# A sixth second-stage product at two levels of Strassen, in a TransNormer attention and StarReLU MLP kernel

## The chip, the cores and the metric

The kernel runs on one core of one Trainium2 chip, in float32 throughout. The metric is the device time of one execution in microseconds (us); a time given is the median of several runs. Five engines with queues of their own work side by side: TensorE (PE) multiplies matrices and writes PSUM, VectorE (DVE) and ScalarE (ACT) do elementwise work, GpSimd (POOL) a little of the set-up, and SyncE (SP) issues nearly all transfers. Each runs its own list of instructions in order, and semaphores make one list wait for another.

## The reference

Batch 8, 8 heads, 576 positions, 64 columns per head, so 4608 tokens of 512 columns; the hidden width is 2048.

```python
kv = einsum('bhsd,bhse->bhde', k, v)
o = einsum('bhsd,bhde->bhse', q, kv)
o = o / sqrt(mean(o * o, axis=-1) + 1e-6) * g_norm
x = o.transpose(0, 2, 1, 3).reshape(4608, 512)
h = x @ w_in                       # 4608x512 @ 512x2048
g = s * max(h, 0)**2 + b
out = g @ w_out                    # 4608x2048 @ 2048x512
```

## The kernel before

The tokens are cut into nine units (U = 9, u from 0) of four chunks of 128 tokens. A unit has a first stage (h and its square, transposed, so that the hidden width lies on partitions), a second stage (the product with w_out), and, between the steps of both, the attention of the following unit.

**First stage (`mm1`).** From unit 1 on it is one level of Strassen-Winograd: seven products in place of eight, for each of NS = 4 blocks s of the hidden width. The products are named x1, z2, x6, y7, x5, x3, y4 after the PSUM bank that they use (x, y, z) and their number. They use sums of the blocks of x (`x_sums`, tiles xs_4 to xs_7) and of w_in (kept from the start). `keep` copies a bank to SBUF on ACT; `relu_sq` squares the positive part on DVE in one operation. For the last block (s = 3) x3 and y4 are put off into the second stage.

**Second stage (`mm2`).** It is also one level of Strassen-Winograd: the products 1 to 7 are of blocks of g (a11, a12, a21, a22 and sums of them, by `G_OF`) with 1024x256 blocks of w_out or sums of those (`w2_dram`). Each is 256 tokens (j = 0, 1 of 128) by 1024 by 256. A direct product (`product`) is eight matrix products of 128x256 for each j, accumulated in one bank. From unit 2 on the products in `TWICE` (1, 2, 6, 7, 4) are split once more by Strassen-Winograd (`second_level`): seven small products m1 to m7, each four matrix products of 128x128, which the trace shows as eight. Their sums of g are made by DVE (`sums`, four 128x512 operations; tiles "sub", eight buffers), their sums of w_out were made once in unit 1 by `parts_of_w` and stored in `w3_dram`. `keep` and `scaled` (line 707) read a bank on DVE, multiply by s and add what is there already. Products 5 and 3 are direct: `x5_of(j)` and `x3(j)`, and both stay in the same x bank, which x5 begins and x3 later ends.

Names of the steps: `p6[3]` is small product m3 of product 6, with its reading. `p4` has product T4 with block a22 of g; its banks are the two of `ps_t` (t_ps) and z. `s2` and `s4` turn g's tiles into Strassen's S2 and S4 in place (S4 stands where a12 was). `with_7` adds product 7 to o2's right half. The results are o1 and o2 (two tiles of 128 tokens each), left and right halves of 256 columns.

**The order of the work** is written out by hand: `rest` lists the second stage in program order, for all engines at once, so the place of a call sets its place in each engine's list. `at(key)` puts in what `sides` gives to that place: steps of the next unit's attention (`turn` transposes q on DVE, `product`, `row_sum`, `norm`, `turn_x`), the loads of q (`loads`, or `loads_in_parts` to spread them), and the sums of x for the next unit. `first[(s, n)]` are places in the first stage, `second[...]` in the second.

**The weights of the second stage** go through a ring of seven tiles. `queue_w2` lists the loads in order, `pump(k)` issues the next k on SP, each into the tile that was used seven places earlier. A direct product has two tiles of 512 KB; a split one has four (2, 2, 2 and 1 of the seven blocks), used in the order 1 2 | 6 7 | 5 3 | 4 (`ORDER`). In units with a batch due, k and v also come through the ring (four tiles).

**SP** takes all of it in program order: ring loads, q, k and v, the stores of w_out's sums in unit 1, and the stores of the results (`store`: four transfers for a tile of 128 tokens, two of them in the first units).

Lines of the profile that matter: 91 (every product), 247 and 250 (additions and subtractions), 409 (transpose of q), 440 (attention product), 547 and 626 (squares on DVE), 592 (`keep` on ACT), 676 and 679 (ring loads, split and direct), 707 (readings), 723 (stores of w_out's sums), 811 (stores of results), 1214 and 1225 (loads of q).

Of the kernel before, what the change touches and what calls it, by code (L numbers as in the profile page):

```python
# [9 lines left out]
FP32 = mybir.dt.float32  # L10
# [6 lines left out]
def kernel(  # L17
# [39 lines left out]
    nc = tc.nc  # L57
# [191 lines left out]
    def sub(o, a, b):  # L249
        nc.vector.tensor_tensor(out=o, in0=a, in1=b, op=ALU.subtract)  # L250
# [38 lines left out]


    w2_dram = [dram.tile([P, FC // 2, HN], FP32, name=f"w2_{i}") for i in range(8)]
    TWICE = (1, 2, 6, 7, 4)
    w3_dram = {
        i: dram.tile([P, 7, FC // 4, P], FP32, name=f"w3_{i}") for i in TWICE
    }
# [212 lines left out]
    def x_sums(u):  # L508
        b11, b12 = xT[u][:, :KH, :TB], xT[u][:, :KH, TB:]
        b21, b22 = xT[u][:, KH:, :TB], xT[u][:, KH:, TB:]  # L510
        for i in (5, 7, 6, 4):
            xs[u, i] = xp.tile([P, KH, TB], FP32, name=f"xs_{i}", tag=f"xs_{i}")

        def t12():
            sub(xs[u, 5], b12, b11)
            sub(xs[u, 6], b22, xs[u, 5])

        def t34():
            sub(xs[u, 7], b22, b12)
            sub(xs[u, 4], b21, xs[u, 6])  # L520

        return t12, t34
# [23 lines left out]
    def relu_sq(t):  # L546
        nc.vector.scalar_tensor_tensor(t, t, 0.0, t, ALU.max, ALU.mult)  # L547
# [38 lines left out]
    def mm1(u, s):  # L586

        st = {}

        def keep(name, src, tag):  # L590
            st[name] = rp.tile([P, 2, TB], FP32, name=name, tag=tag)
            nc.scalar.copy(st[name], src)  # L592

        def x1():
            st["x"] = bank_of("x", "x")
            mm1_product(1, u, s, st["x"], True)
            keep("r1", st["x"], "ra")

        def z2():
            ps = bank_of("z", "z", 1)  # L600
            mm1_product(2, u, s, ps, True)
            t = g_tile("a11", s)
            add(t, ps, st["r1"])
            relu_sq(t)

        def x6():
            mm1_product(6, u, s, st["x"], False)
            keep("r2", st["x"], "rb")

        def y7():  # L610
            st["y"] = bank_of("y", "y")
            mm1_product(7, u, s, st["y"], True)

        def x5():
            mm1_product(5, u, s, st["x"], False)
            keep("r4", st["x"], "ra")
            t = g_tile("a22", s)
            add(t, st["y"], st["r4"])
            relu_sq(t)

        def x3():
            mm1_product(3, u, s, st["x"], False)
            nc.scalar.activation(g_tile("a21", s), st["x"], AF.Relu)  # L623

        def x3_square():
            nc.vector.tensor_mul(ga["a21", s], ga["a21", s], ga["a21", s])  # L626

        def x3_s1():
            g_tile("s1", s)
            g_s1(s)  # L630

        def x3_s3():
            sub(ga["a21", s], ga["a11", s], ga["a21", s])

        def y4():
            mm1_product(4, u, s, st["y"], False)
            add(g_tile("a12", s), st["y"], st["r2"])

        def y4_square():
            relu_sq(ga["a12", s])  # L640

        return dict(
            x1=x1, z2=z2, x6=x6, y7=y7, x5=x5, x3=x3, x3_square=x3_square, x3_s1=x3_s1,
            x3_s3=x3_s3, y4=y4, y4_square=y4_square,
        )
# [13 lines left out]
    queue_w2 = []  # L659
    for u in range(1, U):  # L660
        queue_w2 += [(u, "kv", n) for n in range(NP if u in kv_due else 0)]
        for i in ORDER if u == 1 else (1, 2, 5, 6, 7, 3, 4):
            queue_w2 += [(u, i, n) for n in range(4 if twice(u, i) else 2)]

    def pump(k):
# [21 lines left out]
    def mm2(u, step=None, side={}):  # L687
# [185 lines left out]
            if last(j):  # L873
                store("o2", j, 4 * u + 2 + j, slice(HN, DM))

        def x3(j, *between):
            product(3, j, st["x", j], False)
            for fn in between:
                fn()
            if u > 1:  # L880
                add(right("o1", j), right("o1", j), b_21)
            scaled(rows("o1", j)[:, HN:], st["x", j], b2 if u == 1 else st["o1", j][:, HN:])
            store("o1", j, 4 * u + j)

# [42 lines left out]
        if u == 1:  # L927
            return [
                seq(lambda: x1(0), lambda: parts_of_w(1)),
                seq(lambda: x1(1), lambda: pump(2), s2),  # L930
                seq(lambda: z2(0), lambda: parts_of_w(2)),
                seq(lambda: z2(1), lambda: pump(2), s4),
                seq(lambda: x6(0), lambda: parts_of_w(6)),
                seq(lambda: x6(1), lambda: pump(2)),
                seq(lambda: y7(0), lambda: parts_of_w(7)),
                seq(lambda: y7(1), lambda: pump(2)),
                lambda: x5(0),
                seq(lambda: x5(1), lambda: pump(2)),
                lambda: x3(0),
                seq(lambda: x3(1), lambda: pump(2)),  # L940
                seq(lambda: y4(0), lambda: parts_of_w(4)),
                seq(lambda: y4(1), lambda: pump(2)),
            ]
# [11 lines left out]
            4, lambda j, q: st["r2"][:, j, q], lambda j, q: rows("o2", j)[:, q], "t", "t"  # L955
        )

        def x5_of(j, *between):
            st["x", j] = half(("x", j), "x")
            product(5, j, st["x", j], True)  # L960
            for fn in between:
                fn()
            scaled(right("o2", j), st["x", j], b_21)

        def with_7(j):

            add(right("o2", j), right("o2", j), st["r2"][:, j])
            if last(j):
                store("o2", j, 4 * u + 2 + j, slice(HN, DM))

        def y4_of(j, m):
            p4[m]()
            if last(j):
                store("o2", j, 4 * u + 2 + j, slice(0, HN), (nc.sync, nc.scalar))
            else:
                store("o2", j, 4 * u + 2 + j)

        def rest():
            p1[1]()
            p1[2]()  # L980
            pump(1)
            step["y4"]()
            p1[6]()
            step["y4_square"]()
            p1[7]()
            pump(1)
            p1[5]()
            step["x3"]()
            p2["sums"]()
            p1[3]()  # L990
            pump(1)
            step["x3_square"]()
            p1[4]()
            pump(1)
            at(0)
            p2[1]()
            step["x3_s1"]()
            p2[2]()
            pump(1)
            p2[6]()  # L1000
            step["x3_s3"]()
            p2[7]()
            pump(1)
            s2((0, 1))
            p2[5]()
            x5_of(0, lambda: s2((2, 3)), lambda: p6["sums"]((5, 6)))
            p2[3]()
            pump(1)
            p2[4]()
            pump(1)  # L1010
            at(1)
            x5_of(1, lambda: p6["sums"]((7, 3)), lambda: p7["sums"]((5, 6, 7)))
            pump(2)
            at(2)
            p6[1]()
            s4((0,))
            p6[2]()
            pump(1)
            p6[6]()
            s4((1,))  # L1020
            p6[7]()
            pump(1)
            p6[5]()
            s4((2,))
            st["r2"] = rp.tile([P, 2, HN], FP32, name="or2", tag="rb")
            p7[1]()
            p6[3]()
            pump(1)
            s4((3,))
            p6[4]()  # L1030
            pump(1)
            p7[2]()
            pump(1)
            p7[6]()
            p7[7]()
            pump(1)
            p7[5]()
            at(3)

            def between():  # L1040
                p7["sums"]((3,))
                p4["sums"]()
                at("sums")
                p7[3]()
                pump(1)
                p7[4]()
                pump(1)
                at(("q", 0))
                p4[1]()
                at("norm")  # L1050

            x3(0, between)
            p4[2]()
            p4[6]()
            with_7(0)
            p4[7]()
            with_7(1)
            p4[5]()
            at(4)
            at(5)  # L1060
            x3(1)
            pump(4)
            at(("q", 1))
            y4_of(0, 3)
            pump(1)
            y4_of(1, 4)
            pump(1)
            at(("q", 2))

        return {"sums": p1["sums"], "rest": rest}  # L1070
# [181 lines left out]
    def sides(u):  # L1252
# [34 lines left out]
        else:  # L1287
# [17 lines left out]
                })  # L1305
            else:
                first[2, 0] = [*turn_x[:2], turn[2]]
                first.update({
                    (2, 1): [product[2], row_sum[2]],
                    (2, 2): [norm[2]],  # L1310
                    (2, 3): [turn_x[2], turn[3], *q[1]],
                    (3, 0): [product[3], row_sum[3]],
                    (3, 1): [norm[3]],
                    (3, 2): [turn_x[3]],
                })
        second[5] = [lambda: [sums() for sums in x_sums(u + 1)]]
        return first, second

    for u in range(U):
# [90 lines left out]
```

## Time and profile before

| what | value |
|---|---|
| median of five runs | 954.52 us (952.37, 952.76, 954.52, 955.12, 955.15) |
| the profiled execution's own time | 955.12 us |
| its span | 953.3 us |
| matrix products on TensorE | 7270 |
| mean share of the 16 DMA engines in q1, SP's queue | 54.1% |
| read from and written to HBM | 131.34 MB and 25.95 MB |
| first and last start of TensorE's part in the sixth unit's second stage | 605.63 us and 653.26 us |
| one unit, start of the seventh less start of the sixth | about 100.9 us |

The span is the part of the time that the profiler sees; 1.8 us of this execution lie around it. Busy times of TensorE are modelled and overlap, so the starts of its instructions are the thing to read: the distance between the starts of two groups is what the first costs. A figure in brackets at the end of a line is the time that the engine stood idle just before it, and what ended that. On SP's queue a line's length is the time to issue, not to transfer.

### The profile page before, as it was taken

How to read it: one execution, taken by the hardware profiler on the slowest of the kernel's cores; microseconds unless marked ns; L12 is line 12 of the kernel's file. 1: busy time of each engine (PE TensorE's matmuls, PEld its weight loads, DVE VectorE, ACT ScalarE, POOL GpSimd, SP SyncE). 2: the span in 40 equal slices, each digit the busy share in tenths (PEclk: the TensorE clock that was granted, in tenths of full speed). 3: DMA queues.
4: the chain of work that ended last, by engine and by line, in shares of the span. 5: the costliest groups of instructions: out<-in, count | busy, mean ns of one | idle time of the engine just before them, and what ended most of it. 6: DMA issues, size and time to landing. Idle time of an engine off the chain costs nothing.

```text
span 953.3 us, 17795 instructions
## 1 busy us (share of the span) xinstructions
PE 937.3 (98%) x7270; PEld 840.4 (88%) x7270; DVE 640.1 (67%) x1167; ACT 191.6 (20%) x366; POOL 6.7 (1%) x18
## 2 busy tenths in 40 slices
PE   7999999999999999999999999999999999999997
PEld 7888888888889998889889988999889988998996
DVE  2789667485558765876478656775678567864683
ACT  3684132101221013200231013101320032001100
POOL 2000000000000000000000000000000000000000
PEclk9999999999999999999999999999999999999999
DMA  9588727578762758165644764375526520653064
GB/s 262 185 316 248 249 78 196 136 232 251 211 169 59 245 141 222 22 193 189 178 110 128 240 180 111 92 241 168 154 56 219 189 80 11 221 184 104 26 221 129
DMA packets 136656, 158.46 MB, mean 166 GB/s; under 512 B 77696, under 2 KB 91776, under 8 KB 136448
## 3 DMA queue, kind: packets, MB, share of 16 engines
q1 hardware_dynamic: 133472, 155.57, 54.1%
q10 hardware_dynamic: 2784, 1.77, 0.8%
q8 instruction: 57, 0.93, 0.4%
q14 instruction: 23, 0.19, 0.1%
q0 software_dynamic: 320, 0.00, 0.0%
HBM read 131.34 MB, written 25.95 MB: 165 GB/s over the span
## 4 chain that ended last, share of the span: by engine, by line
PE 87%; DVE 5%; DMA 4%; ACT 2%; issue 1%; SPq 0%; DVEq 0%; ACTq 0%
PE x_ps L91 40%; PE y_ps L91 25%; PE z_ps L91 8%; PE t_ps L91 8%; PE x_ps L440 3%; DMA w_sb<-w 2%; PE kv_ps L377 2%; DMA w_raw<-in_moe_w_in_dram 1%; ACT xT L494 1%; DMA kv_sb<-in_k_dram 1%; DVE xT L488 1%; DVE a L247 1%; DVE a L547 1%; DVE xn L463 1%; DVE sub L250 0%
## 5 line engine op out<-in xcount | busy, mean ns | idle before, releaser
L592 ACT COPY r<-x_ps 128x512 f32<-128x512 f32 x96 | 56.0, 584 | 406.2 <-PE x_ps L91 384.0
L91 PE MATMUL x_ps<-xs,ws 128*128 128x256 f32 x512 | 122.1, 381 | 0.8 <-ACT r L592 0.4
L91 PE MATMUL y_ps<-xs,wb 128*128 128x256 f32 x512 | 122.6, 382 | 0.3 <-DVE a L247 0.3
L91 PEld LDWEIGHTS x_ps<-xs,ws 128*128 128x128 f32 x512 | 96.4, 190 | 15.9 <-ACT r L592 2.9
L91 PEld LDWEIGHTS y_ps<-xs,wb 128*128 128x128 f32 x512 | 95.5, 190 | 16.1 <-DVE a L247 2.6
L247 DVE TENSOR_TENSOR a<-y_ps,r 128x512 f32<-128x512 f32 x64 | 43.9, 686 | 72.2 <-ACT r L592 60.1
L91 PE MATMUL x_ps<-xT,wa 128*128 128x256 f32 x384 | 89.8, 380 | 0.1
L91 PEld LDWEIGHTS x_ps<-xT,wa 128*128 128x128 f32 x384 | 72.2, 190 | 10.5 <-issue 0.6
L91 PE MATMUL x_ps<-w_sb,a 128*128 128x256 f32 (+1 forms) x376 | 80.0, 365 | 0.8 <-DMA w_sb<-w 0.8
L91 PEld LDWEIGHTS x_ps<-w_sb,a 128*128 128x128 f32 x376 | 66.8, 190 | 9.6 <-DMA w_sb<-w 1.2
L547 DVE SCALAR_TENSOR_TENSOR a<-a 128x512 f32<-128x512 f32 x96 | 66.4, 692 | 3.1
L91 PE MATMUL y_ps<-w_sb,sub 128*128 128x128 f32 x504 | 62.0, 275 | 0.0
L91 PEld LDWEIGHTS y_ps<-w_sb,sub 128*128 128x128 f32 x504 | 60.2, 192 | 0.7
L91 PE MATMUL x_ps<-xT,ws 128*128 128x256 f32 x256 | 60.5, 379 | 0.0
L91 PE MATMUL z_ps<-xT,wa 128*128 128x256 f32 x256 | 60.5, 379 | 0.0
L91 PE MATMUL x_ps<-w_sb,s 128*128 128x256 f32 x256 | 58.2, 380 | 1.3 <-DMA w_sb<-w 1.3
L91 PE MATMUL t_ps<-w_sb,sub 128*128 128x128 f32 x448 | 54.8, 275 | 0.0
L91 PEld LDWEIGHTS z_ps<-xT,wa 128*128 128x128 f32 x256 | 48.6, 190 | 6.6
L91 PEld LDWEIGHTS x_ps<-w_sb,s 128*128 128x128 f32 x256 | 47.4, 190 | 7.9 <-DMA w_sb<-w 1.2
L626 DVE TENSOR_TENSOR a<-a 128x512 f32<-128x512 f32 x32 | 22.1, 690 | 47.9 <-ACT a L623 47.9
L91 PE MATMUL y_ps<-w_sb,a 128*128 128x128 f32 (+1 forms) x360 | 53.7, 298 | 0.0
L91 PEld LDWEIGHTS x_ps<-xT,ws 128*128 128x128 f32 x256 | 48.1, 190 | 6.3
(139 smaller groups left out, 1267.2 us busy)
## 6 DMA issues: line engine op xcount, KB each, us to landing
w_sb<-w SPq DMA_DIRECT2D x147, 512.0 KB, 4.8
w_sb<-w SPq DMA_DIRECT2D x35, 256.0 KB, 2.8
w_raw<-in_moe_w_in_dram SPq DMA_DIRECT2D x8, 1024.0 KB, 7.3
w_raw<-in_moe_w_out_dram SPq DMA_DIRECT2D x8, 1024.0 KB, 5.2
w_sb<-in_k_dram SPq DMA_DIRECT2D x48, 144.0 KB, 2.9
w_sb<-in_v_dram SPq DMA_DIRECT2D x48, 144.0 KB, 3.0
out_dram<-o SPq DMA_DIRECT2D x104, 64.0 KB, 2.6
w<-sub SPq DMA_DIRECT2D x20, 256.0 KB, 4.3
```

The source lines that it names most:

```text
L91: nc.tensor.matmul(o, lhsT=lhsT, rhs=rhs, start=start, stop=stop, skip_group_check=True)
L247: nc.vector.tensor_tensor(out=o, in0=a, in1=b, op=ALU.add)
L377: nc.tensor.matmul(ps[r][l * HB : l * HB + HB, i, :], lhsT=kv[l][rows, 0, j, :], rhs=kv[l][rows, 1, j, :], start=(j == 0), stop=(j == R - 1),)
L440: nc.tensor.matmul(ps[32 * p : 32 * p + 32, w, :], lhsT=st["qT"][:, p, 32 * w : 32 * w + 32], rhs=bd_kv[(b if w < 2 else b1) % 2][:, p, :] ...
L463: nc.vector.tensor_tensor(out=st["xn"].rearrange("p h d -> p (h d)").rearrange("p (c h e) -> p h c e", c=KC, h=H), in0=st["x"].rearrange(" ...
L488: nc.vector.transpose(out=to, in_=st["xn"].rearrange("p h d -> p (h d)").rearrange("p (c x) -> p c x", c=KC))
L494: nc.scalar.activation(to[:, i], to[:, i], AF.Copy, scale=g_col[:, i : i + 1])
L547: nc.vector.scalar_tensor_tensor(t, t, 0.0, t, ALU.max, ALU.mult)
L592: nc.scalar.copy(st[name], src)
L626: nc.vector.tensor_mul(ga["a21", s], ga["a21", s], ga["a21", s])
```

## The change

- Product 3 (S4 with block B22 of w_out) joins `TWICE`: in unit 1 `parts_of_w(3)` makes and stores its sums; from unit 2 on it is split in seven (`p3`, banks x, y and z). The order of the ring is ... 7, 4, 3, so product 4 comes ahead of product 3, and product 5 no longer stays in its bank: `with_5` adds it from o2's right half, where `x5_of` puts it.
- The sums of products 4 and 3 (and the last of 7) are no longer made in one run but one or two at a time between the readings, and `s4` is grouped otherwise.
- In the last block of the first stage, from unit 2 on, the two squares are done by ACT, and a21's is ahead of p2's sums.
- The two pairs of `x_sums` are at two places (5 and 6).
- In the last unit the results are stored by halves for both j: o2's right and o1's left half after `with_7(j)`, o2's left after `p4[4]`, o1's right after `p3[3]` and `p3[4]`, on SP and ACT in turn.
- In unit 3 the transpose of the fourth chunk comes ahead of the third's product, the row sum one place later, and the second half of q's loads is in four parts.

```diff
-    TWICE = (1, 2, 6, 7, 4)
+    TWICE = (1, 2, 6, 7, 4, 3)
...
         def t12():
+            tiles(5, 6)
             sub(xs[u, 5], b12, b11)
             sub(xs[u, 6], b22, xs[u, 5])
 
         def t34():
+            tiles(7, 4)
             sub(xs[u, 7], b22, b12)
             sub(xs[u, 4], b21, xs[u, 6])
...
             add(t, st["y"], st["r4"])
-            relu_sq(t)
+            if u > 1 and s == NS - 1:
+                nc.scalar.activation(t, t, AF.Relu)
+                nc.scalar.square(t, t)
+            else:
+                relu_sq(t)
...
         def x3_square():
-            nc.vector.tensor_mul(ga["a21", s], ga["a21", s], ga["a21", s])
+            if u > 1 and s == NS - 1:
+                nc.scalar.square(ga["a21", s], ga["a21", s])
+            else:
+                nc.vector.tensor_mul(ga["a21", s], ga["a21", s], ga["a21", s])
...
-        for i in ORDER if u == 1 else (1, 2, 5, 6, 7, 3, 4):
+        for i in ORDER if u == 1 else (1, 2, 5, 6, 7, 4, 3):
...
-        def x3(j, *between):
+        def x3(j):
             product(3, j, st["x", j], False)
-            for fn in between:
-                fn()
-            if u > 1:
-                add(right("o1", j), right("o1", j), b_21)
...
-                lambda: x3(0),
+                seq(lambda: x3(0), lambda: parts_of_w(3)),
...
+        p3 = second_level(3, lambda j, q: right("o1", j, q), lambda j, q: right("o1", j, q), "x")
...
+        def with_5(j):
+
+            add(right("o1", j), right("o1", j), right("o2", j))
+
         def with_7(j):
 
             add(right("o2", j), right("o2", j), st["r2"][:, j])
-            if last(j):
+            if u == U - 1:
                 store("o2", j, 4 * u + 2 + j, slice(HN, DM))
...
+                store("o1", j, 4 * u + j, slice(0, HN))
+
+        def store_o2(j):
+            store("o2", j, 4 * u + 2 + j, slice(0, HN if u == U - 1 else DM))
+
+        def store_o1(j):
+            cols, queues = (slice(HN, DM), (nc.sync, nc.scalar)) if u == U - 1 else (slice(0, DM), (nc.sync, nc.sync))
+            store("o1", j, 4 * u + j, cols, queues)
...
             step["x3"]()
+            step["x3_square"]()
             p2["sums"]()
...
             p6[1]()
-            s4((0,))
             p6[2]()
...
-            s4((1,))
             p6[7]()
             pump(1)
+            s4((0, 1))
             p6[5]()
+            st["r2"] = rp.tile([P, 2, HN], FP32, name="or2", tag="rb")
             s4((2,))
...
+            p7["sums"]((3,))
+            p4["sums"]((5,))
             p7[5]()
+            p4["sums"]((6,))
             at(3)
-
-            def between():
-                p7["sums"]((3,))
-                p4["sums"]()
-                at("sums")
-                p7[3]()
-                pump(1)
-                p7[4]()
-                pump(1)
-                at(("q", 0))
-                p4[1]()
-                at("norm")
-
-            x3(0, between)
+            p4[1]()
+            p7[3]()
+            pump(1)
+            with_5(0)
+            p7[4]()
+            pump(1)
+            at("sums")
+            p4["sums"]((7,))
+            at(("q", 0))
             p4[2]()
+            pump(1)
             p4[6]()
+            at("norm")
+            p4[7]()
+            pump(1)
+            p4["sums"]((3,))
+            p3["sums"]((5,))
+            p4[5]()
+            with_5(1)
+            p3["sums"]((6,))
+            p3[1]()
+            at(4)
+            p4[3]()
+            pump(1)
+            at(("q", 1))
+            p3["sums"]((7,))
+            p3[2]()
+            p3[6]()
+            p3[7]()
+            p3["sums"]((3,))
             with_7(0)
-            p4[7]()
+            p3[5]()
             with_7(1)
-            p4[5]()
-            at(4)
             at(5)
-            x3(1)
-            pump(4)
-            at(("q", 1))
-            y4_of(0, 3)
-            pump(1)
-            y4_of(1, 4)
-            pump(1)
+            p4[4]()
+            for j in range(2):
+                store_o2(j)
+            pump(3)
+            p3[3]()
+            store_o1(0)
+            pump(1)
+            p3[4]()
+            store_o1(1)
+            pump(1)
+            at(6)
             at(("q", 2))
...
                 first[2, 0] = [*turn_x[:2], turn[2]]
+                parts = loads_in_parts(5, 1, 4)
+                second["q", 0], second["q", 1] = [parts[2]], [parts[3]]
                 first.update({
-                    (2, 1): [product[2], row_sum[2]],
-                    (2, 2): [norm[2]],
-                    (2, 3): [turn_x[2], turn[3], *q[1]],
+                    (2, 1): [turn[3], product[2]],
+                    (2, 2): [row_sum[2], norm[2], *parts[:2]],
+                    (2, 3): [turn_x[2]],
...
-        second[5] = [lambda: [sums() for sums in x_sums(u + 1)]]
+        second[5], second[6] = [[lambda n=n: x_sums(u + 1)[n]()] for n in range(2)]
```

More of the change, by code (lines that the diff above doesn't have):

```diff
@@ L510, in x_sums, with tiles @@
         b21, b22 = xT[u][:, KH:, :TB], xT[u][:, KH:, TB:]
-        for i in (5, 7, 6, 4):
-            xs[u, i] = xp.tile([P, KH, TB], FP32, name=f"xs_{i}", tag=f"xs_{i}")
+        def tiles(*which):
+            for i in which:
+                xs[u, i] = xp.tile([P, KH, TB], FP32, name=f"xs_{i}", tag=f"xs_{i}")
         def t12():
+            tiles(5, 6)
             sub(xs[u, 5], b12, b11)
@@ L963, in x5_of @@
             scaled(right("o2", j), st["x", j], b_21)
+        def with_5(j):
+            add(right("o1", j), right("o1", j), right("o2", j))
         def with_7(j):
             add(right("o2", j), right("o2", j), st["r2"][:, j])
-            if last(j):
+            if u == U - 1:
                 store("o2", j, 4 * u + 2 + j, slice(HN, DM))
[L971 to L976, printed above, removed]
+                store("o1", j, 4 * u + j, slice(0, HN))
[4 more added lines that the diff above has]
+            store("o1", j, 4 * u + j, cols, queues)
         def rest():
@@ L991, in rest @@
             pump(1)
-            step["x3_square"]()
             p1[4]()
@@ L1019, in rest @@
             p6[6]()
-            s4((1,))
             p6[7]()
             pump(1)
+            s4((0, 1))
             p6[5]()
+            st["r2"] = rp.tile([P, 2, HN], FP32, name="or2", tag="rb")
             s4((2,))
-            st["r2"] = rp.tile([P, 2, HN], FP32, name="or2", tag="rb")
             p7[1]()
```

## The prediction

> **What bounds the kernel now.** I read the page first (which engine is full), then TensorE's timeline of one steady unit, then its few waits, then the SP queue at the end. Measurement tells about 0.2% (1.9 us) from no change.
>
> Page, part 1, and part 4:
> ```profile
> PE 937.3 (98%) x7270; PEld 840.4 (88%) x7270; DVE 640.1 (67%) x1167; ACT 191.6 (20%) x366; POOL 6.7 (1%) x18
> ...
> PE 87%; DVE 5%; DMA 4%; ACT 2%; issue 1%; SPq 0%; DVEq 0%; ACTq 0%
> ```
> TensorE is the bound: anything it no longer streams is gained, if nothing makes it wait.
>
> Timeline of TensorE, sixth unit (start, us, engine, operation):
> ```profile
> 636.53 2.84 PE L91 MATMUL y_ps<-w_sb,sub 128*128 128x128 f32 x24
> 639.21 3.62 PE L91 MATMUL x_ps<-w_sb,a 128*128 128x256 f32 x16
> 642.67 1.05 PE L91 MATMUL y_ps<-w_sb,sub 128*128 128x128 f32 x8
> ```
> The printed lengths overlap; starts count. One row tile of the direct third product takes 642.67 - 639.21 = 3.46 us, three small products 639.21 - 636.53 = 2.68, so one "slot" is 0.893 us. No gap lies between: this unit has no wait.
>
> Timeline of TensorE, the waits (in brackets) of the fourth and ninth units:
> ```profile
> 386.17 1.99 PE L91 MATMUL x_ps<-xs,ws 128*128 128x256 f32 x8 [0.39 <-ACT r L592]
> 388.76 1.08 PE L440 MATMUL x_ps<-bd_kv,qT 128*32 128x128 f32 x32 [0.60 <-DVE qT L409]
> ...
> 416.84 1.97 PE L91 MATMUL x_ps<-w_sb,s 128*128 128x256 f32 x8 [0.54 <-DMA w_sb<-w]
> 419.60 1.99 PE L91 MATMUL x_ps<-w_sb,s 128*128 128x256 f32 x8 [0.80 <-DMA w_sb<-w]
> ...
> 934.25 1.99 PE L91 MATMUL x_ps<-w_sb,a 128*128 128x256 f32 x8 [0.85 <-DMA w_sb<-w]
> ```
> These 3.18 us are nearly all the waits in seven two-level units.
>
> SP's queue, fourth unit and end; TensorE's last product:
> ```profile
> 373.70 38.28 SPq L1214 DMA_DIRECT2D q_sb<-in_q_dram  x64
> ...
> 946.50 4.55 SPq L811 DMA_DIRECT2D out_dram<-o  x10
> ```
> ```profile
> 946.67 1.06 PE L91 MATMUL t_ps<-w_sb,a 128*128 128x128 f32 x8
> ```
> The 64 loads of q block SP until 411.98, when ring loads due from about 402.9 go out; that is the wait of 416 to 420. At the end TensorE is done at 946.67 + 0.89 = 947.56, the span only at 953.3: 5.74 us of tail. SP issues ten stores at 0.455 us each up to 951.05, and 2.25 us later all has ended.
>
> **The parts and their cost**, against the profiled execution (span 953.3, its time 955.12; the median is 0.6 lower).
>
> *1. The product.* Direct: 2 x 3.455 = 6.91 us. At two levels: 7 x 0.893 = 6.25. Gain 0.66 in each of seven units: **-4.6 us**. It lies on the path wholly.
>
> *2. DVE.* Per unit four sums (0.60 to 0.72 from start to start), seven readings of 128x128 (0.35) instead of two of 128x256 (0.48), two additions of o2 in place of two of b_21 (0.42 both): 2.7 + 2.45 - 0.96 = +4.2; two squarings (0.69 each) go to ACT, so +2.8 of about 101 us, at 67% busy. ACT gets three 0.59 us operations for it and is 20% busy. What matters is when. I laid DVE's list in the new order beside the slots, counting from p6[1]; a reading starts 0.20 after its product ends (t_ps, 647.13 to 647.33). p4[1] is slot 12, p3[1] slot 19, p3[4] slot 27, end 25.0. The tightest: the sum for p3[7] is done at 20.2, its slot starts at 20.54; the reading that frees x_ps for p3[6] ends at 19.25, its slot starts 19.64. So nothing waits, with 0.3 us to spare: 0 in five units (without that cover, a wait of up to 0.5 per unit). The sums of x now come one pair after the slots, done at 27.4; the next unit needs the first pair at 28.4 and the second at 30.2. In the third unit DVE has a row sum (0.68), a reciprocal and multiply (0.9) and a transpose (0.7) besides in this stretch, TensorE only 1.1 of attention product: p4[3] waits some 0.4 for the reading of p4[5] and p3[7] some 0.45 for its sum; the same stretch lost about 0.2 before: **+0.6** (0 to 1.5).
>
> *3. Ring loads.* 26 tiles per unit, not 24. A load goes out when the tile seven places earlier is free. The tightest distance was 6.0 us (second half of product 3: free after p6[3]); the load of the last unit took 6.97 and cost the 0.85. Now the tightest is 8 slots, 7.14 us. Nearest rows: that load with three others behind it, 6.97. **-0.85** (0 to -0.85), and no new wait; later tiles of p3 are issued behind fewer bytes.
>
> *4. Fourth unit.* SP takes 16 + 24 loads of q in the first stage, not 64: done by about 399, before the ring needs it; 12 more at each of two later places, where a load of 256 KB stands behind 12 x 0.47 = 5.6 us and still lands about 0.6 ahead of p3[4]. So 0.54 + 0.80 go. The transpose of chunk 19 is laid two steps earlier, into DVE's idle 2.14 us ahead of 380.78: the 0.60 goes. The row sum (384.17) no longer stands ahead of the addition that ACT's copy waits for: the 0.39 goes. **-2.3** (0 to -2.3).
>
> *5. Second unit.* Four subtractions fit in DVE's idle 2.97 us ahead of 240.00. But seven more stores of 256 KB enter SP's queue, ahead of two loads, a store and q for the unit after next; seven such took 254.57 to 260.53 on SP. SP hardly idles from 225 to 289, so all behind is 4 to 7.5 us late: the loads of q for the third unit's third chunk, last issued by 276.05, land near 282 to 286 (2.5 us landing) where the transpose stood at 283.93 and TensorE took it at 284.86. The k and v loads (landed by 254, needed at 267) have room. **+0.5** (0 to +2.3).
>
> *6. The end.* Before, 18 stores of the last unit were on SP, and the first eight were out by 943.8. Now o1 and o2 of the last unit are stored in halves: with_7(0) releases eight, with_7(1) eight, o2's left halves eight, o1's right halves four on SP and four on ACT: 28 on SP, none before with_7(0). That addition stands on DVE behind the reading of p3[6] and a sum: 20.74 + 0.3 + 0.6 + 0.4 = 22.05, which is 2.95 ahead of TensorE's end. 28 x 0.455 = 12.7, so SP is done 9.8 after TensorE's end and the span at 9.8 + 2.25 = 12.0, where it was 5.74: **+6.2**. Bounds: by the shorter of the two stores on ACT's queue (0.36) 28 cost 10.1, and the term is +3.7; by q's loads (64 in 38.28, 0.60 each with their waits) 16.8, and it is +10. I take 0.455: same queue, same source, half rows too (four at 942.03 went at the same pace).
>
> A rule weighs here. The Trainium skill, "DMA: Bandwidth & Descriptors", section "Issuing engines are not separate DMA queues", says that issuing from several engines saves only the time to initiate a DMA, usually small beside the DMA itself. By that the ten extra stores would cost nearly nothing and the sum would be near -6.6. This trace shows 0.455 us to initiate beside 1.6 us to land for 32 KB, one after the other on one queue, so the row decides.
>
> **Sum:** -4.6 + 0.6 - 0.85 - 2.3 + 0.5 + 6.2 = **-0.45** on 955.12, 954.7; on the median of 954.52 it is **954.0**, no change that can be told.
>
> **Rivals.**
> *A, faster: the stores at the end cost less.* If one takes 0.36, the term is +3.7 and the time 954.0 - 2.5 = 951.5; if the tail did not grow at all, 947.8. For it: the shortest single issue of a store was 314 ns. Against: ten in a row at 0.455 in the same place. It decides from below 0.40 us per store.
> *B, slower: DVE becomes the bound in p4 and p3.* Slots 12 to 25 hold some eight sums (0.65), fifteen readings (0.32 from start to start) and four additions, 5.2 + 4.8 + 1.6 = 11.6 of 12.5 us, with x's sums on top. If one product per unit waits 0.5 in all seven, +3.5: 957.5. It decides from 0.35 per unit. For it: spares of 0.3 only. Against: in p1 and p2 DVE was as dense (612.67 to 617.7 without a gap) and TensorE did not wait.
> *C: the second unit's stores make SP late at the upper end:* +2.3 instead of +0.5, 955.8, still no change. For it: no slack on SP; against: 3.4 us of waits within the q loads may absorb it.
> *D: the old waits stay* (new loads of q, denser ring): 954.0 + 3.1 = 957.1, slower. For it: more ring bytes per us in p6 to p3; against: longer distances.
>
> **How the numbers follow.** Forecast 0.36, A 0.30, B 0.18, C 0.07, D 0.09. Faster is A, 0.30; same is forecast and C, 0.43; slower B and D, 0.27. The range holds all but the far end of A (tail not grown) and two rivals together: 950.5 to 958.0; the forecast's own is 952.7 to 956.3.
>
> **What would show it.** Small products per unit up by seven at 0.893 spacing, each unit without kv or waits some 0.66 shorter (step 1). No bracket ahead of p3 products in units 4 to 9, one or two near 0.4 in the third (2). No DMA wait near 416 and in the last unit (3, 4). A later transpose near 284 (5). Tail of 12 us with SP issuing 28 stores without a gap (6). Wrong if the tail stays near 6, or if small products in p4 and p3 start with waits in every unit.

## The result and the profile after

The changed kernel takes 955.77 us (median of 32 runs, 953.99 to 958.58) against 953.67 for the kernel before (54 runs, 951.82 to 955.31): ratio 1.0024, 95% interval 1.0019 to 1.0029. It is slower by 2.1 us; the forecast was no change, 954.0. All times here are of executions at nearly the full granted clock (0.993 and more); one at 0.848, 1078.07 us in `w3_act_again`, is not counted.

The page after, parts 1 and 4, as shown of before:

```profile
PE 933.0 (98%) x7438; PEld 842.2 (88%) x7438; DVE 657.6 (69%) x1220; ACT 204.9 (21%) x387; POOL 6.7 (1%) x18
...
PE 86%; DVE 5%; DMA 4%; ACT 2%; SPq 1%; issue 1%; DVEq 0%; ACTq 0%
```

TensorE has 4.3 us less to do, and yet the span grew from 953.3 to 954.5. In the chain of work that ended last SP's queue has risen from 0% to 1%.

TensorE's timeline after, sixth unit, from p7[6], p7[7] and p7[5] to the start of the next unit:

```profile
634.78 2.84 PE L91 MATMUL y_ps<-w_sb,sub 128*128 128x128 f32 x24
637.46 1.06 PE L91 MATMUL t_ps<-w_sb,a 128*128 128x128 f32 x8
...
643.71 1.06 PE L91 MATMUL x_ps<-w_sb,a 128*128 128x128 f32 x8
644.61 1.06 PE L91 MATMUL t_ps<-w_sb,sub 128*128 128x128 f32 x8
645.50 1.06 PE L91 MATMUL z_ps<-w_sb,a 128*128 128x128 f32 x8
...
650.86 1.06 PE L91 MATMUL y_ps<-w_sb,a 128*128 128x128 f32 x8
651.75 0.60 PE L91 MATMUL x_ps<-xT,wa 128*128 128x256 f32 x2
```

Start to start is 0.89 throughout, with no wait: the sixth product is split, and DVE keeps up.

TensorE's timeline after, the waits of the third and fourth units:

```profile
277.81 1.08 PE L440 MATMUL x_ps<-bd_kv,qT 128*32 128x128 f32 x32 [0.47 <-DVE qT L409]
...
286.27 1.08 PE L440 MATMUL x_ps<-bd_kv,qT 128*32 128x128 f32 x32 [0.28 <-DVE qT L409]
...
387.37 1.99 PE L91 MATMUL x_ps<-xs,ws 128*128 128x256 f32 x8 [0.39 <-ACT r L596]
...
450.12 1.13 PE L91 MATMUL y_ps<-w_sb,a 128*128 128x128 f32 x8 [0.36 <-DMA w_sb<-w]
```

The waits near 388, 416, 420 and 934 are gone; that of 0.39 stayed; two on q in the third unit and one on a ring load at the end of the fourth are new.

The end, TensorE's last product and SP's queue after (line 822 is `store` here):

```profile
941.22 1.06 PE L91 MATMUL y_ps<-w_sb,a 128*128 128x128 f32 x8
```
```profile
939.16 13.11 SPq L822 DMA_DIRECT2D out_dram<-o  x28
```

TensorE ends at 941.22 + 0.89 = 942.11, 5.45 us earlier than before (947.56). SP starts its stores at 939.16 and issues 28 in a row, 0.468 each, until 952.27; the span ends 2.2 later. The tail is 12.39, where it was 5.74.

The length of each unit, from the start of its first product to that of the next unit's (us, one profiled execution each; the last unit is counted to TensorE's end):

| kernel | second | third | fourth | fifth | sixth | seventh | eighth | last | tail |
|---|---|---|---|---|---|---|---|---|---|
| before | 105.19 | 101.85 | 103.78 | 100.92 | 100.90 | 100.90 | 97.97 | 94.53 | 5.74 |
| after | 105.24 | 102.53 | 101.32 | 100.41 | 100.26 | 100.27 | 97.32 | 92.77 | 12.39 |

From the fifth to the eighth unit the difference is 0.51 to 0.65, close to the predicted 0.66. What does not fit it is in the third, the fourth and the last unit, and in the tail.

### The profile page after: what moved, and what is told of

The parts are those of the page before. It is cut to its first block, busy times and chain, and to the rows that moved or that the text cites. A ratio compares the mean times of both kernels' runs of the same rounds, so it can differ in the third digit from the quotient of the medians.

```text
span 954.5 us, 18263 instructions
## 1 busy us (share of the span) xinstructions
PE 933.0 (98%) x7438; PEld 842.2 (88%) x7438; DVE 657.6 (69%) x1220; ACT 204.9 (21%) x387; POOL 6.7 (1%) x18
## 4 chain that ended last, share of the span: by engine, by line
PE 86%; DVE 5%; DMA 4%; ACT 2%; SPq 1%; issue 1%; DVEq 0%; ACTq 0%
PE x_ps L91 37%; PE y_ps L91 26%; PE z_ps L91 9%; PE t_ps L91 8%; PE x_ps L440 3%; PE kv_ps L377 2%; DMA w_sb<-w 1%; DMA w_raw<-in_moe_w_in_dram 1%; ACT xT L494 1%; DMA kv_sb<-in_k_dram 1%; DVE xT L488 1%; SPq L1246 1%; DVE a L247 1%; DVE sub L250 1%; DVE a L551 1%
## 5 line engine op out<-in xcount | busy, mean ns | idle before, releaser
L91 PE MATMUL y_ps<-w_sb,sub 128*128 128x128 f32 x560 | 69.5, 275 | 0.1
L91 PEld LDWEIGHTS y_ps<-w_sb,sub 128*128 128x128 f32 x560 | 66.4, 192 | 0.6 <-DVE sub L250 0.3
L551 DVE SCALAR_TENSOR_TENSOR a<-a 128x512 f32<-128x512 f32 x89 | 61.5, 691 | 2.8
L91 PE MATMUL y_ps<-w_sb,a 128*128 128x128 f32 (+1 forms) x416 | 61.2, 295 | 0.4 <-DMA w_sb<-w 0.4
L91 PEld LDWEIGHTS y_ps<-w_sb,a 128*128 128x128 f32 x416 | 55.4, 192 | 2.7 <-DVE xs L250 0.5
L91 PEld LDWEIGHTS t_ps<-w_sb,sub 128*128 128x128 f32 x448 | 52.3, 192 | 0.2
L637 DVE TENSOR_TENSOR a<-a 128x512 f32<-128x512 f32 x25 | 17.3, 691 | 46.7 <-ACT a L631 46.7
```

The source lines that it names most:

```text
L91: nc.tensor.matmul(o, lhsT=lhsT, rhs=rhs, start=start, stop=stop, skip_group_check=True)
```

## The experiments

My theory on the record was: the split product gives 4.6, the order of q about 2.3, and the stores at the end take it back. The rivals were that the end is not set by SP's issuing, and that the waits of the one profiled execution of before are not those of a typical one.

### The stores at the end

`tail_early`: o1's left halves, done since p2, are stored behind the last ring load.

```diff
-                store("o1", j, 4 * u + j, slice(0, HN))      # in with_7
...
             p4[2]()
             pump(1)
+            if u == U - 1:
+                for j in range(2):
+                    store("o1", j, 4 * u + j, slice(0, HN))
```

> The changed kernel, but in the last unit the left halves of o1 (done since p2) are stored behind the last ring load, ahead of with_7. Theory (SP's issue of stores makes the end): 20 instead of 28 stores stand on SP behind with_7(0); at 0.468 us each the tail after TensorE's end falls from 12.4 to 8.7 us and the time by 3.7, from 955.8 to about 952.0. Rival (the end is set by when the last stores can start or by landing, not by issuing): tail and time stay, 955.8.

Measured: 951.94 (11 runs), ratio 0.9983 (0.9972 to 0.9995); tail 8.70. Eight stores fewer behind with_7(0) took 3.7 us off the tail and 3.8 off the time: 0.46 each, as predicted for one issue. The rival falls.

`tail_both`: in addition all other stores of the last unit go in turn to SP and ACT.

```diff
-                store("o2", j, 4 * u + 2 + j, slice(HN, DM))
+                store("o2", j, 4 * u + 2 + j, slice(HN, DM), (nc.sync, nc.scalar))
...
-            store("o2", j, 4 * u + 2 + j, slice(0, HN if u == U - 1 else DM))
+            cols, queues = (slice(0, HN), (nc.sync, nc.scalar)) if u == U - 1 else (slice(0, DM), (nc.sync, nc.sync))
+            store("o2", j, 4 * u + 2 + j, cols, queues)
```

> As the one before, and all the last unit's stores behind with_7 in turn on SP and ACT. Theory: ten stores on each queue, SP done about 2.6 us after TensorE's end, tail about 5.0 us, time about 948.4, faster than both kernels (ratio to before 0.9945). Rival (both queues share the transfer engines, so a second queue gives nothing): tail 8.7 as with half of it, 952.0.

Measured: 949.34 (5 runs), ratio 0.9958 (0.9944 to 0.9972); tail 5.72. A second queue does help. SP's and ACT's queues of this kernel at the end:

```profile
931.74 13.37 SPq L822 DMA_DIRECT2D out_dram<-o  x20
```
```profile
938.95 6.21 ACTq L822 DMA_DIRECT2D out_dram<-o  x12
```

I had counted ten stores per queue behind with_7(0); there are twelve, and ACT takes 0.52 for one. Both end at 945.1, 3.2 after TensorE, so the tail is 0.7 longer than expected.

`before_tail`: the same turn of queues for the last unit of the kernel before.

```diff
-            store("o1", j, 4 * u + j)
+            store("o1", j, 4 * u + j, queues=(nc.sync, nc.scalar) if u == U - 1 else (nc.sync, nc.sync))
...
-                store("o2", j, 4 * u + 2 + j, slice(HN, DM))
+                store("o2", j, 4 * u + 2 + j, slice(HN, DM), (nc.sync, nc.scalar))
...
-                store("o2", j, 4 * u + 2 + j)
+                store("o2", j, 4 * u + 2 + j, queues=(nc.sync, nc.scalar) if u == U - 1 else (nc.sync, nc.sync))
```

> The kernel before with the last unit's stores (18 on SP, 2 on ACT) in turn on both queues, nothing else. Theory (SP's issue ends the kernel before too): the stores behind the last products halve, the tail falls from 5.74 to about 4.0 and the time by 1.7. Rival: the tail before is set by the last product's own store, nothing changes.

Measured: 952.57, ratio 0.9989 (0.9979 to 1.0); tail 4.74, 1.0 less instead of 1.7. The interval reaches 1.0, so in the time the gain is not clear of nothing; the tail shows it. Its unit lengths are those of before but for the fourth (104.56), and there is no wait in the last unit (93.42).

### The fourth unit's order of q

`q_only`: the kernel before with the hunk in `sides` alone.

```diff
+                parts = loads_in_parts(5, 1, 4)
+                second["q", 0], second["q", 1] = [parts[2]], [parts[3]]
...
-                    (2, 1): [product[2], row_sum[2]],
-                    (2, 2): [norm[2]],
-                    (2, 3): [turn_x[2], turn[3], *q[1]],
+                    (2, 1): [turn[3], product[2]],
+                    (2, 2): [row_sum[2], norm[2], *parts[:2]],
+                    (2, 3): [turn_x[2]],
```

> The kernel before with the fourth unit's new order of q alone (loads in four parts, transpose of chunk 19 and row sum moved). Theory (the waits of the profiled execution are in every execution): the waits of 0.60, 0.54 and 0.80 go, the fourth unit is 2.5 us shorter (a wait costs somewhat more than its bracket), time 2.5 below before, 951.2. Rival (that execution had more waits on transfers than most): the unit in the profile is shorter, but the median falls by 1.3 or less.

Measured: 951.51 (11 runs), ratio 0.9978 (0.9969 to 0.9988), that is 1.1 to 3.0 us. TensorE's timeline of this kernel's fourth unit:

```profile
385.05 2.00 PE L91 MATMUL x_ps<-xs,ws 128*128 128x256 f32 x8 [0.39 <-ACT r L592]
387.09 1.08 PE L440 MATMUL x_ps<-bd_kv,qT 128*32 128x128 f32 x32
...
414.46 3.62 PE L91 MATMUL x_ps<-w_sb,s 128*128 128x256 f32 x16
```

The wait for the transpose and both for the ring are gone, the one for ACT is not; the unit has 101.54, 2.2 to 3.1 less than in three profiles with the old order. The median fell by 1.9, between the theory's 2.5 and the rival's 1.3, and the interval holds both: the gain is there in the times, its size only roughly.

`before_again`: the kernel before, unchanged, for a second profile.

> The kernel before once more, unchanged, for a second profile. Theory (the execution on which the prediction's sum stood had waits on transfers that are not in every one): the wait of 0.85 in the last unit and some 0.5 us at the start are missing, and its own time is nearer 953.5. Rival (the waits are always there): fourth unit 103.8, last unit 94.5, time near 955.

Measured: 955.47. TensorE's waits in its fourth unit:

```profile
389.29 1.08 PE L440 MATMUL x_ps<-bd_kv,qT 128*32 128x128 f32 x32 [0.60 <-DVE qT L409]
...
417.85 1.97 PE L91 MATMUL x_ps<-w_sb,s 128*128 128x256 f32 x8 [1.03 <-DMA w_sb<-w]
420.95 2.00 PE L91 MATMUL x_ps<-w_sb,s 128*128 128x256 f32 x8 [1.14 <-DMA w_sb<-w]
```

The rival holds for the fourth unit, whose waits are there again and larger (unit 104.60), and for the time. The theory holds for the last unit, whose wait is missing (93.42), but not for the start, where nothing was missing: the second unit began at 142.20, before at 141.52. Of five profiles in which product 3 is direct (before, this, `before_tail`, `q_only`, `before_q_tail`) only the one the prediction stood on has it.

### The second unit's stores and the loads of q behind them

`after_again`: the changed kernel, unchanged.

> The changed kernel once more, unchanged, for a second profile. The tail is 12.4 again and the units from the fifth on 100.25; if the waits on q in the third unit (0.9 us) depend on the execution, they may be missing as in the profile with the early stores, and the third unit is 101.85 instead of 102.5.

Measured: 957.48; tail 12.49. The third unit has 105.28, more than in the first profile, not less. DVE's transpose waits for q and TensorE for DVE (two answers, DVE and TensorE):

```profile
277.43 0.71 DVE L409 STREAM_TRANSPOSE qT<-q_sb 128x512 f32<-128x512 f32 x1 [4.16 <-DMA q_sb<-in_q_dram]
```
```profile
278.28 1.08 PE L440 MATMUL x_ps<-bd_kv,qT 128*32 128x128 f32 x32 [1.97 <-DVE qT L409]
279.29 3.68 PE L91 MATMUL y_ps<-xs,wb 128*128 128x256 f32 x8
282.77 1.93 PE L91 MATMUL x_ps<-xs,ws 128*128 128x256 f32 x8
```

Not all of the 105.28 is waiting. From 279 to 283 the granted clock of TensorE was 0.57 in this execution, and the product at 279.29 took 3.48 from start to start; in the first profile the clock was 1.00 from 277 to 281 and the same product took 280.65 - 278.82 = 1.83. So 1.65 us of this unit are the clock. Whether the wait just before brought it on is not shown.

SP's queue in the changed kernel's first profile shows what stands ahead of those loads:

```profile
245.47 1.19 SPq L734 DMA_DIRECT2D w<-w_sb  x2
246.75 1.93 SPq L734 DMA_DIRECT2D w<-sub  x3
248.74 0.66 SPq L734 DMA_DIRECT2D w<-w_sb  x1
249.49 0.69 SPq L734 DMA_DIRECT2D w<-sub  x1
...
271.52 1.84 SPq L1257 DMA_DIRECT2D q_sb<-in_q_dram  x4
273.40 9.80 SPq L1246 DMA_DIRECT2D q_sb<-in_q_dram  x16
```

The seven new stores take 245.47 to 250.18, and the loads that began at 264.80 and 266.68 before begin 6.7 later.

`w3_act`: those seven stores are issued by ACT.

```diff
-                nc.sync.dma_start(out=w3_dram[i][:, n], in_=t)
+                (nc.scalar if i == 3 else nc.sync).dma_start(out=w3_dram[i][:, n], in_=t)
```

> The changed kernel with the seven stores of product 3's sums of w_out in the second unit issued by ACT instead of SP. Theory (SP's list made the loads of q late): no wait on the transposes in the third unit, which is 0.9 us shorter, time 954.9. Rival (the transfers themselves are slow there, 1.8 MB more to write): the loads of q still land late, 955.8.

Measured: 955.30 (12 runs), ratio 1.0021 (1.0011 to 1.0032): not separated from the changed kernel. The profile: third unit 101.65, no wait on q (TensorE's timeline):

```profile
277.43 1.08 PE L440 MATMUL x_ps<-bd_kv,qT 128*32 128x128 f32 x32
285.54 1.08 PE L440 MATMUL x_ps<-bd_kv,qT 128*32 128x128 f32 x32
```

So I ran both once more, on one chip: `after_third` is the changed kernel, `w3_act_again` the version with ACT.

> The changed kernel unchanged, beside the next one on the same chip. Theory (SP's late loads of q cost about 1.5 us in the mean of its executions, 0.2 to 3.6): 955.8, and in the profile the third unit is 101.9 to 105.

> The stores of product 3's sums on ACT, once more, on the same chip as the unchanged one. Theory: 1.0 to 1.5 us below it, third unit 101.65 without waits on q. Rival (these waits are rare, their mean is below 0.5): within 0.5 us of it.

Measured: 956.20 (6 runs), ratio 1.0036 (1.0023 to 1.0050), and 954.44 (11 runs), ratio 1.0014 (1.0003 to 1.0026): 1.8 us apart, a little more than the theory's 1.0 to 1.5, though the two intervals overlap a little. In the profile of `after_third` the third unit has 102.27 and the fourth 102.73, 2.0 more than with ACT; most of that is the wait for the ring load behind q (TensorE's timeline):

```profile
448.05 1.06 PE L91 MATMUL x_ps<-w_sb,sub 128*128 128x128 f32 x8
450.81 1.13 PE L91 MATMUL y_ps<-w_sb,a 128*128 128x128 f32 x8 [1.71 <-DMA w_sb<-w]
```

All profiles, third and fourth unit:

| product 3's sums stored by | third unit | fourth unit |
|---|---|---|
| SP: `after`, `tail_early`, `tail_both`, `after_again`, `after_third` | 102.53, 101.85, 102.77, 105.28, 102.27 (mean 102.94) | 101.32, 100.72, 101.58, 100.79, 102.73 (mean 101.43) |
| ACT: `w3_act`, `w3_act_again`, `best`, `best_rows` | 101.65, 101.49, 101.65, 101.57 (mean 101.59) | 100.73, 100.72, 100.79, 100.73 (mean 100.74) |

With ACT there is no such wait in any of four profiles. With SP four of five have one on q in the third unit (`tail_early` has none), and three a ring wait in the fourth; against the mean with ACT the units are longer by 0.3 to 3.7 (mean 1.35, of it 0.33 the clock in `after_again`) and by 0 to 2.0 (mean 0.7). That SP's list makes q late is shown in the third unit; the times put the gain of taking the stores off SP at 0.5 and 1.8 us in the two pairs, of which only the second was run on one chip, so its size in a typical run is known only to about that. Why the fourth unit's ring wait went too was not separated: two of the four ACT versions also have q's part behind the ring load, the other two do not, and two of the five SP versions were free of it.

### Versions that beat both

`best`: the changed kernel with the edits of `tail_both` and `w3_act`, and

```diff
-            at(("q", 0))
             p4[2]()
             pump(1)
+            at(("q", 0))
+            if u == U - 1:
+                with_7(0)
+                for j in range(2):
+                    store("o1", j, 4 * u + j, slice(0, HN))
             p4[6]()
...
-            with_7(0)
+            if u < U - 1:
+                with_7(0)
+            else:
+                with_7(1)
             p3[5]()
-            with_7(1)
+            if u < U - 1:
+                with_7(1)
```

> The changed kernel with the early stores of o1, both queues at the end, with_7(0) of the last unit ahead of p4[6] and with_7(1) ahead of p3[5], the stores of product 3's sums on ACT, and q's third part behind the ring load that it stood ahead of. Theory: tail about 5.0 instead of 5.7, no waits on q in the third unit and none on the ring in the fourth: 1.0 to 1.5 below the version with both queues alone, 948.1, ratio to before 0.9945. Rival (what is left over against the sum is not in these places): 949.3, as that version.

Measured: 946.99 (6 runs), ratio 0.9928 (0.9913 to 0.9944): 6.3 us faster than before on the same chip (953.27). The waits in the third and fourth unit are gone; the tail did not shrink: 6.35. The gain over `tail_both` is 2.35 where 1.0 to 1.5 was expected: between the two profiles the third and fourth units give 1.9 and the start of the second unit 0.7, and the longer tail takes 0.6 back.

`before_q_tail`: the kernel before with `q_only` and `before_tail` together.

> The kernel before with the fourth unit's new order of q and the last unit's stores in turn on both queues: everything that helps and needs no sixth split product. Theory (the parts add): -2.0 and -0.9, 950.4; against it the split product in the mended version (946.99) is worth 3.4. Rival (the split product brings nothing in the time, and all of the mended version's gain is order and stores): as the mended version, 947.0.

Measured: 949.66 (6 runs), ratio 0.9967 (0.9954 to 0.9979). The parts add. Against `best_rows` below, run on the same chip (946.89, intervals apart), the split product and what goes with it are worth 2.8 us; against `best`, on another chip, 0.0039 of the time or 3.7 us. The rival, that the product brings nothing, falls. What goes with it (the squares on ACT, the new places of the sums) was not tried alone.

`best_rows`: `best` with with_7 at its old places and o2 of the last unit in whole rows.

```diff
-            if u == U - 1:
-                store("o2", j, 4 * u + 2 + j, slice(HN, DM), (nc.sync, nc.scalar))
...
+            queues = (nc.sync, nc.scalar) if u == U - 1 else (nc.sync, nc.sync)
+            store("o2", j, 4 * u + 2 + j, queues=queues)
```

> The mended version, but with_7 at its old places and o2 of the last unit stored in whole rows behind p4[4], in turn on both queues: eight stores per queue behind with_7 instead of twelve on SP. Theory (the number of stores to issue makes the end): tail 5.0 instead of 6.35, time 945.7. Rival (a transfer that starts later ends later, the number does not matter): 947 or above.

Measured: tail 4.15, the shortest of all, with eight stores on ACT and sixteen on SP in all; time 946.89 (5 runs), ratio 0.9935 (0.9923 to 0.9947), the same as `best` within the intervals. The tail speaks for the number of stores; in the time it doesn't show, and in this profile the second unit began 2.4 us later than in that of `best` (143.14 against 140.70), where the two kernels do not differ. Part of it is likely the clock: from 20 to 40 us the granted clock was 0.91 here and 1.00 in `best`, and the product that starts at 37.07 in `best` starts at 38.72 here, so 1.65 of the 2.4 us had come about by then.

## Why the prediction was wrong

The range held the time (950.5 to 958.0); the direction did not hold. What bounds the kernel and where the edit pays and costs was seen rightly; what failed is the size of four terms, steps 3 to 6, above all the wait of the last unit, counted as a gain of 0.85 and worth 0.2, and the second unit's stores, put at 0.5 and measured at 1.35. The time of rival C, 955.8, was met by luck: its term alone came to 1.35 of the 2.3 us that it stands for. Step by step:

- **Step 1, the product, -4.6: right.** 0.63 to 0.65 from the sixth unit on, leaving out the wait in the last: 97.97 to 97.32, 93.42 to 92.77.
- **Step 2, DVE: right.** No wait for DVE in p4 and p3 from the fourth unit on. In the third, free of q's waits, the unit fell by only 101.74 - 101.59 = 0.15 instead of 0.65 (mean of the five versions with a direct product 3, mean of the four with ACT): +0.5 for the predicted +0.6. In the timeline it lies in small delays, the largest ahead of p3[7], which starts 345.19 - 344.05 = 1.14 after p3[6] where a slot has 0.89. Rival B, DVE as the bound, did not come.
- **Step 3, the last unit's wait, -0.85: wrong.** It was in one profile of five, where it cost 94.53 - 93.42 = 1.1; as a mean that is -0.2. I took a wait of one execution for a property of the kernel.
- **Step 4, the fourth unit, -2.3: half right.** The order of q gave 103.78, 104.60 and 104.56 to 101.54 and 101.53, that is -2.8 in the profiles and -1.9 in the median of `q_only`; only the 0.39 stayed. But the sentence that the 256 KB ring load "still lands about 0.6 ahead of p3[4]" was wrong: the twelve loads of q ahead of it took 7.43 on SP instead of 5.6, and TensorE waited in three of five profiles, +0.7 in the mean. The line, SP's queue of the changed kernel:

```profile
439.43 7.43 SPq L1257 DMA_DIRECT2D q_sb<-in_q_dram  x12
446.97 0.38 SPq L687 DMA_DIRECT2D w_sb<-w  x1
```

- **Step 5, the second unit, +0.5: mechanism right, size wrong.** SP was late by 6.7, inside the 4 to 7.5 predicted; it hit the transpose of the second chunk first, where I had looked at the third. Mean +1.35 in five profiles (+1.0 without the slowed clock in `after_again`), above the bound of 2.3 in that one.
- **Step 6, the end, +6.2: right, a little small.** Tails of 12.39, 12.49 and 12.34 against 5.74 and 5.78: +6.65. SP took 0.468 for a store instead of 0.455, which over 28 is 0.36; it started 942.11 - 939.16 = 2.95 ahead of TensorE's end, exactly as laid out. The rule of the Trainium skill that was weighed there (page "DMA: Bandwidth & Descriptors", section "Issuing engines are not separate DMA queues") would have left the tail as it was; eight stores moved took 3.8 us off the time, so here the time to initiate is not small.

The sum with the measured terms is -4.6 + 0.5 - 0.2 - 2.8 + 0.7 + 1.35 + 6.65 = +1.6; the medians say +2.1 and the ratio 1.8 to 2.8. The 0.2 to 1.2 left over is no more than the third unit alone differs between executions, and is not explained further. Against the predicted -0.45 the four terms of steps 3 to 6 were all sized too favourably, by 0.65, 0.2, 0.85 and 0.45: each is a transfer queue, and each time I took the quick value.

## What to carry to other kernels

A gain on the engine that is the bound arrived almost in full here (0.63 to 0.65 of 0.66 us in a unit without waits), but look at what else the edit puts on the queues: a tail 6.65 us longer, made by 28 stores issued one by one with none of them early, took back more than the split product gave. Another place and a second queue give it back. When a serial queue has no slack, cost each new entry by the spacing of its own rows when the transfers are busy, and look for the first reader that it makes late. A wait seen in one execution is a sample: take a second profile, or halve it, before it is counted as a gain.

## What was not expected of the hardware

The same kernel's waits on transfers differ much from one execution to the next: the third unit of the changed kernel took between 102.27 and 105.28 in three profiles with the same instructions (1.65 of that the clock), while its fifth to seventh units, without such waits, repeat within 0.2 us.

TensorE's granted clock is not the same in every execution either. From 20 to 40 us it was 0.91 in five of the 14 profiles (`before`, `after`, `before_again`, `w3_act`, `best_rows`) and 1.00 in the other nine, and in `after_again` it was 0.57 from 279 to 283 us. What decides it is not shown.

Stores that SP issued beside ring loads were slow. In `best` SP's queue has

```profile
935.40 1.75 SPq L822 DMA_DIRECT2D out_dram<-o  x1
```

against a median of 0.39 for its 20 stores, which took 929.35 to 942.93. Between them SP also stood still until ring loads had landed: 2.5 us in two waits in `best` (the longer 2.1), 1.7 us in two in `tail_both`. So the early place of stores is not free of cost; that this is what kept the tail of `best` at 6.35 is likely but was not tested, and what held up the store of 1.75 was not looked into.
